# A RetNet layer and an RWKV channel mix on one core: the hand-written order of all instructions behind the first score products is replaced by another one

## The chip, the core and the metric

The kernel runs on one core of one Trainium2 chip. The metric is the device time of one execution in microseconds (us); a kernel is run several times and the median counts. Engines: PE is TensorE, DVE is VectorE, ACT is ScalarE, POOL is GpSimd, SP is SyncE.

## The reference

A decaying recurrent attention gives `x`, and a channel mix with a gate works on it. Batch 4, 8 heads, 768 tokens, head width 64, model width 512, inner width 1024.

```python
def _attn_ref(q, k, v):
    gamma = 1.0 - 2.0 ** (-5.0 - np.arange(H))
    for t in range(S):
        state = gamma * state + outer(k[:, :, t], v[:, :, t])   # per batch and head
        y[:, :, t] = 1/sqrt(D) * q[:, :, t] @ state

def _moe_ref(x, mu_k, mu_r, w_k, w_v, w_r):
    x_prev = x shifted by one token, zeros first
    xk = mu_k * x + (1.0 - mu_k) * x_prev
    xr = mu_r * x + (1.0 - mu_r) * x_prev
    k = np.maximum(xk @ w_k, 0.0)
    v = k * k @ w_v
    r = 1.0 / (1.0 + np.exp(-(xr @ w_r)))
    return r * v
```

## The kernel before

The 4 x 768 tokens are cut into 12 blocks of 256 tokens, three to a batch (blocks 0 to 2 are batch 0, and so on). A block goes through two parts. In the first the recurrence is done in chunks: q and k are turned, scores are made within a chunk and masked, and a state is summed and handed to the next block of the same batch. The second part mixes each token with the one before it, multiplies by `w_k`, takes relu and square, multiplies by `w_v`, and gates the result with a sigmoid of the product with `w_r`. Blocks 3 and 4, 6 and 7, 9 and 10 go through the mix and the product with `w_k` as pairs (`GROUPS`), so their product is 512 tokens wide and one word K stands for both.

There is no loop over blocks and no scheduler. The text `ORDER` lists some 620 words, each of which issues one step; the program walks it from left to right (the last loop of the kernel) under a manual schedule. Each engine and each DMA queue executes its own steps strictly in the order of the text, and waits, in the order of its queue, for what the step at its head depends on: its inputs, and that the buffer or PSUM bank it writes has been read by its last user. So the relative place of two words on one engine decides which of them can hold up the other. A word is `code.arguments`, then `~v`, `~a`, `~p` or `~s` for an engine (DVE, ACT, POOL, SP), then `@` and the PSUM banks. The codes that matter here, with the line of the step in the profile:

- `lq lk lv` (lines 265, 270): load q, k, v of a block; on POOL's queue except two on SP. Q and K have rings of four buffers, so `lv.10` needs `vs.6` to be done. `wk wr wv`: the weights, in parts.
- `tq tk` (L388): DMA transposes of q and k on SP's queue, for blocks 8 to 11. Blocks 0 to 7 use PE: `Tq Tk` (L343, 348, 354), copied out of PSUM by `Eq Ek` on ACT (L276).
- `vs` (L291, DVE): v scaled. `S` (L412, 425, 433, PE): scores. `M` (L457, DVE): mask. `C` (L469, 487, PE): products of k and v for the state. `U` (L522, DVE): the state's running sum. `G` (L527 ACT, L531 DVE): its decay.
- `I`, `Y`, `J` (L544, 574, 590, 601, PE): what the carried state and the masked scores give to the output. `sy` (L276, ACT): a small read of the output's bank.
- `D` (L633, 640, DVE): the attention's result leaves PSUM. `dx` (L655, DVE): difference to the token before. `X.n.0.j` and `X.n.1.j` (L681, DVE): the mix for `w_k` and for the gate, one quarter of the width each.
- `K` (L695 pairs, L705 single, PE): product with `w_k`. `Qa` (L727, ACT): relu. `Qb` (L741, L745, ACT): square. `R` (L754, PE): product with `w_r`. `s` (L760, ACT): sigmoid. `V` (L766; `Vc` L784 at the very end, PE): product with `w_v`, in two halves. `O` (L772; `Oc` L791, DVE): the result. `st` (L779; `sc` L799, on SP's queue, the last on ACT's): the store, from a ring of four buffers.
- `z` (L840, 847, PE): products of zeros, into a bank whose content is not used, placed where PE would have nothing to do. The argument counts quarter passes.

Of the kernel before, what the change touches and what calls it, by code (L numbers as in the profile page):

```python
# [50 lines left out]
Qb.2.1~a X.2.1.3 U.4.2 V.1.0.0@3 M.4 V.0.0.1 U.4.3 dx.3~v Tq.7@67 I.4@45 V.0.1.1 lq.11~p sy.4~a  # L51
O.0.0 Y.4 st.0.0 O.0.1 V.1.0.1 D.4~v lk.6~p st.0.1 R.2.0@2 O.1.0 V.1.1.1 s.2.0 lk.7~p dx.4~v
Eq.7~a V.2.0.0@1 O.1.1 Tk.5@23 Tq.5@67 lv.6~p X.3.0.0 Tq.6@45 R.2.1@0 X.3.0.3 Eq.6~a X.3.0.2
V.2.0.1 Ek.5~a lv.7~p X.3.0.1 V.2.1.0@4 G.4~a vs.5~v V.2.1.1 Eq.5~a X.3.1.3 K.3.7@5 lq.10~p s.2.1
# [14 lines left out]
K.6.0@5 Qa.6.5~a D.8~v Qb.6.1~a R.6.0@7 Qb.6.7~a dx.8~v R.7.1@4 K.6.3@2 O.5.0 s.7.1 Qa.6.0~a  # L69
X.8.0.3 R.6.1@3 X.8.0.0 Qb.6.0~a X.8.0.2 R.7.0@6 Qa.6.3~a X.8.0.1 U.9.0~a K.8.2@2 s.6.1 U.9.1  # L70
X.8.1.1 Qb.6.3~a K.8.3@3 U.9.2 Qa.8.2~a X.8.1.0 Qb.6.5~a K.8.1@5 vs.11~v s.7.0 V.6.1.0@2 s.6.0
U.9.3 Qa.8.1~a G.9~v C.10@01 X.8.1.3 Qa.8.3~a I.9@67 S.9@45 U.10.0~v V.6.1.1 Qb.8.3~a M.9 K.8.0@3
O.6.1 V.6.0.0@4 U.10.1 Qa.8.0~a st.6.1 U.10.2 st.5.0 Qb.8.2~a S.10@23 tq.11~s U.10.3 Y.9 Qb.8.0~a
M.10 I.10@01 Qb.8.1~a V.7.0.0@5 sy.10~a st.5.1 D.9~v V.6.0.1 tk.11~s V.8.1.0@2 X.8.1.2 dx.9~v Y.10
C.11@67 V.8.1.1 D.10~v V.8.0.0@3 dx.10~v V.8.0.1 V.7.0.1 X.9.0.2 R.8.1@0 X.9.0.3 X.9.0.1 V.7.1.0@1
s.8.1 X.9.0.0 V.7.1.1 O.8.1 K.9.7@0 O.6.0 st.8.1 G.10~v K.9.0@2 O.7.1 U.11.0~v K.9.5@4 Qa.9.0~a
O.7.0 K.9.2@1 X.9.1.2 Qb.9.0~a st.7.0 st.6.0 Qa.9.7~a X.9.1.1 K.9.1@5 U.11.1 X.9.1.0 K.9.6@0
Qa.9.1~a X.9.1.3 Qb.9.7~a R.8.0@2 Qa.9.6~a K.9.3@5 s.8.0 Qb.9.1~a R.10.0@0 O.8.0 Qa.9.2~a U.11.2
# [861 lines left out]
```

## Time and profile before

| | |
|---|---|
| median of 3 runs | 154.9 us (153.5, 154.9, 155.57) |
| the profiled execution | 153.46 us, of which its span 151.7 us |
| mean granted TensorE clock | 0.993 |
| PE busy | 142.4 us, 94% of the span |
| DVE busy | 126.7 us, 84% |
| ACT busy | 90.5 us, 60% |
| POOL busy | 61.2 us, 40% |
| DMA | 24.39 MB, mean 161 GB/s |

The span runs from the first to the last instruction of the program that the profiler recorded. Busy shares of PE count a matmul until its modelled end, so a busy PE is not PE at its peak. In rows of groups the columns are the line, the engine, the operation, out<-in, the shape and the count, then the busy time and the mean duration of one in ns, then the engine's idle time before them and who ended it. A row of the timeline has its start and its length in us, and in brackets the idle time before it and its releaser; several instructions of a kind are merged, with their count behind the x. "issue" as a releaser is time in which the engine waited for nothing that the profile shows. A row of stages has the stretch, its length, then busy time and number of instructions of each engine, the granted clock, the DMA share and the traffic. A row of the chain has start, length and what ran.

### The profile page before, as it was taken

To read this page: it belongs to the slowest core of one execution; us is meant where nothing else is said; L and a number is where in the kernel's file an instruction comes from. 1 tells how busy PE (TensorE), PEld (TensorE's weight loads), DVE (VectorE), ACT (ScalarE), POOL (GpSimd) and SP (SyncE) were. 2 spreads that over 40 slices of the span, in tenths; PEclk is the share of its full clock that TensorE was granted. 3 is DMA by queue.
4 is the path that set the end of the run, shared out by engine and by line. 5 is a ranking of instruction groups with operands and counts; after the bars stand their busy time and mean duration, and the time that the engine had idled before them with its cause. 6 is when DMAs were issued, how large, how long until landed. Compare 5 with 4: busy or idle time off the path is not lost.

```text
span 151.7 us, 5268 instructions
## 1 busy us (share of the span) xinstructions
PE 142.4 (94%) x2285; PEld 81.1 (53%) x2285; DVE 126.7 (84%) x208; ACT 90.5 (60%) x176; POOL 61.2 (40%) x76
## 2 busy tenths in 40 slices
...
GB/s 142 249 239 192 181 240 235 163 195 211 197 191 193 178 170 249 249 257 216 160 189 222 236 107 267 167 6 4 117 179 58 69 138 138 6 0 0 114 167 138
DMA packets 57599, 24.39 MB, mean 161 GB/s; under 512 B 49128, under 2 KB 53096, under 8 KB 57576
## 3 DMA queue, kind: packets, MB, share of 16 engines
...
q8 instruction: 18, 0.29, 0.8%
q10 hardware_dynamic: 432, 0.32, 0.7%
...
## 4 chain that ended last, share of the span: by engine, by line
PE 63%; DMA 15%; DVE 12%; issue 4%; POOL 3%; ACT 0%; DVEq 0%; POOLq 0%
PE ps L766 23%; PE ps L695 11%; PE ps L754 10%; DMA v<-in_v_dram 10%; PE ps L705 9%; DMA wk<-in_moe_w_k_dram 5%; DVE dx L655 2%; DVE xk L681 2%; PE ps L544 2%; PE ps L469 2%; DVE a L457 2%; PE ps L574 2%; PE ps L343 1%; PE ps L412 1%; DVE xr L681 1%
## 5 line engine op out<-in xcount | busy, mean ns | idle before, releaser
L766 PE MATMUL ps<-wv,k2s 128*128 128x512 f16 x184 | 43.0, 379 | 0.0
L727 ACT ACTIVATE kr<-ps 128x512 f32<-128x512 f32 x48 | 28.1, 596 | 22.8 <-PE ps L695 12.9
L766 PEld LDWEIGHTS <-k2s 128*128 128x128 f16 x184 | 17.4, 98 | 19.5 <-issue 0.2
L754 PE MATMUL ps<-wr,xr 128*128 128x512 f16 x96 | 23.4, 379 | 0.0
L705 PE MATMUL ps<-xk,wk 128*128 128x256 f16 x192 | 22.8, 273 | 0.4 <-DVE xk L681 0.4
L695 PE MATMUL ps<-xk,wk 128*128 128x512 f16 x96 | 22.7, 380 | 0.0
L457 DVE TENSOR_TENSOR a<-ps,c_sb 128x1024 f16<-128x1024 f32 (+1 forms) x18 | 19.5, 1099 | 3.7 <-PE ps L412 3.6
L760 ACT ACTIVATE rs<-ps 128x512 f32<-128x512 f32 x24 | 13.8, 608 | 13.9 <-PE ps L754 13.6
L772 DVE SCALAR_TENSOR_TENSOR os<-ps,rs 128x512 f32<-128x512 f32 x23 | 15.4, 685 | 6.7 <-DMA out_dram<-os 4.7
L705 PEld LDWEIGHTS <-wk 128*128 128x128 f16 x192 | 18.4, 98 | 4.1 <-DVE xk L681 0.5
L270 POOL DMA_DIRECT2D v<-in_v_dram x20 | 17.9, 919 | 6.0 <-DVE vs L291 4.6
L681 DVE SCALAR_TENSOR_TENSOR xr<-dx,mu,xT 128x256 f16<-128x256 f32 (+1 forms) x36 | 19.6, 566 | 0.1
L681 DVE SCALAR_TENSOR_TENSOR xk<-dx,mu,xT 128x256 f16<-128x256 f32 (+1 forms) x36 | 18.6, 567 | 0.1
L270 POOL DMA_DIRECT2D k<-in_k_dram x20 | 17.8, 917 | 1.4 <-DMA v<-in_v_dram 0.9
L291 DVE TENSOR_TENSOR vs<-v,csm_sb 128x1024 f16<-128x1024 f32 x12 | 14.6, 1217 | 3.2 <-DMA v<-in_v_dram 3.2
L741 ACT ACTIVATE k2s<-kr 128x512 f16<-128x512 f32 x24 | 14.8, 632 | 0.2
L655 DVE TENSOR_TENSOR dx<-xT 128x1024 f32<-128x1024 f32 x12 | 14.6, 1220 | 0.1
L695 PEld LDWEIGHTS <-wk 128*128 128x128 f16 x96 | 9.0, 98 | 10.3
L754 PEld LDWEIGHTS <-xr 128*128 128x128 f16 x96 | 9.0, 98 | 9.9
L745 ACT ACTIVATE k2s<-kr 128x512 f16<-128x512 f32 x24 | 14.1, 630 | 0.2
L633 DVE TENSOR_TENSOR xT<-ps,gy_sb 128x512 f32<-128x512 f32 x16 | 11.0, 689 | 2.3 <-PE ps L544 1.2
L270 POOL DMA_DIRECT2D q<-in_q_dram x10 | 9.0, 921 | 7.1 <-PE ps L343 6.8
...
## 6 DMA issues: line engine op xcount, KB each, us to landing
out_dram<-os SPq DMA_DIRECT2D x23, 256.0 KB, 4.0
v<-in_v_dram POOLq DMA_DIRECT2D x20, 256.0 KB, 6.6
k<-in_k_dram POOLq DMA_DIRECT2D x21, 128.0 KB, 6.9
q<-in_q_dram POOLq DMA_DIRECT2D x6, 256.0 KB, 8.7
q<-in_q_dram POOLq DMA_DIRECT2D x11, 128.0 KB, 6.6
v<-in_v_dram POOLq DMA_DIRECT2D x2, 512.0 KB, 6.9
wv<-in_moe_w_v_dram POOLq DMA_DIRECT2D x2, 512.0 KB, 9.2
wk<-in_moe_w_k_dram POOLq DMA_DIRECT2D x2, 256.0 KB, 8.8
```

Source lines behind the costliest of these rows:

```text
L270: e.dma_start(out=to[:, i, hs], in_=src[:, i])
L291: e.tensor_tensor(out=VS(n), in0=V32(n).rearrange("p (h i d) -> p i h d", i=2, h=H), in1=gks[:, int(half(n) or wide(n)), :, :, None].to_br ...
L457: nc.vector.tensor_tensor(out=dst, in0=dst if n in SPLITM else src, in1=mask[:, None, None, :].to_broadcast(list(dst.shape)), op=ALU.mult,)
L655: e.tensor_tensor(out=DX(k)[:, :, m * TM + t0 : m * TM + t1], in0=x[:, :, c + t0 : c + t1], in1=x[:, :, c - 1 + t0 : c - 1 + t1], op=ALU.s ...
L681: nc.vector.scalar_tensor_tensor(out=XM[w](k)[:, j, t0:t1], in0=DX(k)[:, j, t0:t1], scalar=mu[:, w * NCO + j : w * NCO + j + 1], in1=x[:, ...
L695: nc.tensor.matmul(banks("K", n, g), lhsT=wk16[:, co, g * P : g * P + P], rhs=XM[0](k)[:, co, :], start=(co == 0), stop=(co == NCO - 1),)
L705: nc.tensor.matmul(pz[:, i, :], lhsT=wk16[:, co, fo * P : fo * P + P], rhs=XM[0](k)[:, co, m * TM + t0 : m * TM + t1], start=(i == 0 and c ...
L727: nc.scalar.activation(out=kr, in_=banks("K", n, g, *u), func=AF.Relu)
L741: nc.scalar.activation(out=k2s[:, n % 3 : n % 3 + 2, g, :], in_=kr, func=AF.Square,)
L754: nc.tensor.matmul(banks("R", n, tb), lhsT=XM[1](k)[:, co, t : t + P], rhs=wr16[:, co, :], start=(co == 0), stop=(co == NCO - 1),)
L766: nc.tensor.matmul(banks("V", n, tb), lhsT=K2(n)[:, fo, tb * P : tb * P + P], rhs=wv16[:, fo, :], start=(fo == 0), stop=(fo == NFO - 1),)
L772: nc.vector.scalar_tensor_tensor(out=OS(2 * n + tb), in0=banks("V", n, tb), scalar=1.0 / (KSC * KSC), in1=RS(2 * n + tb), op0=ALU.mult, op ...
```

## The change

All words from the second line of the first score products on stand in another order, and many have other PSUM banks. The operations are the same ones with the same operands, and the loads are kept: each engine has the same work, with these exceptions. The zero products in the changed part have the counts 2, 2, 8 and 1 in place of 4, 3 and 5, and two more of the small reads `sy` are made on ACT (blocks 7 and 11). POOL's queue has its loads in the same sequence up to block 6; behind `lv.7` it goes on with `lq.8` and `lk.8` ahead of `lv.10`. SP's queue has `tk.9 tk.8 tq.8 tq.9` where it had `tq.8 tk.8 tq.10`, and its stores in another order. The diff, cut to the front, the two stretches around blocks 5 to 8, and the end:

```diff
@@ -35,54 +35,54 @@
 lq.0.0.2~s lk.0.0.2~s lv.0~p mu~s lk.0.2.4~p gy.0~v lq.0.2.4~p lv.1~p cq.0.0.2~a lk.1~p z.8@7
 Tq.0.0.2@0 ck.0.0.2~a lq.1~p Eq.0.0.2~a lq.2~p z.3@7 Tk.0.0.2@1 Ek.0.0.2~a wk.1~p gy.1~a z.3@7
 S.0.0.0.2@01 S.0.1.0.2@23 vs.0~v Tk.0.2.4@4 M.0.0.0.2 Ek.0.2.4~a z.1@7 Tq.0.2.4@5 lk.2~p C.0@67
-M.0.1.0.2 Eq.0.2.4~a U.0.0~v z.1@4 S.0.1.2.4@45 I.0@23 U.0.1 S.0.0.2.4@01 M.0.1.2.4 G.0~a
-M.0.0.2.4 vs.1~v wk.0~p z.4@6 Y.0 mt@0 Tk.1@1 D.0~v me C.1@45 Ek.1~a Tq.1@0 U.1.0~v dx.0~v Eq.1~a
-U.1.1 z.3@7 I.1@01 S.1.1@23 X.0.0.3 Tq.2@4 M.1.1 S.1.0@67 lv.2~p Eq.2~a M.1.0 wr~p X.0.0.0 z.5@5
-Y.1 X.0.0.1 X.0.0.2 Tk.2@6 D.1~v K.0.3@7 Ek.2~a X.0.1.2 lv.3~p Qa.0.3~a S.2.0@01 dx.1~v S.2.1@45
-G.1~a K.0.2@7 X.0.1.0 Qb.0.3~a K.0.0@6 X.1.0.2 Qa.0.2~a X.1.0.0 lq.3~p X.1.0.1 K.0.1@2 Qa.0.0~a
-X.0.1.3 X.1.0.3 Qb.0.2~a X.0.1.1 K.1.1@3 M.2.1 lk.3~p K.1.2@6 Qa.1.1~a vs.2~v K.1.3@7 Qb.1.1~a
-lk.4~p Qa.1.2~a X.1.1.0 K.1.0@3 Qa.1.3~a X.1.1.3 M.2.0 C.2@7 Qa.1.0~a lq.4~p R.0.1@6 Qb.1.2~a
-U.2.0~v Qb.0.0~a X.1.1.1 I.2@01 Y.2 vs.3~v sy.2~a Qb.1.0~a lv.4~p J.2 Tq.3@7 Qa.0.1~a D.2~v
-R.0.0@3 s.0.1 Eq.3~a wv.0~p X.1.1.2 C.3@45 Tk.3@6 dx.2~v U.3.0~a R.1.1@7 Qb.1.3~a lq.7~p Ek.3~a
-U.3.1 R.1.0@2 wv.1~p X.2.0.2 X.2.0.3 s.1.1 lk.5~p S.3.0@45 X.2.0.1 s.0.0 S.3.1@01 X.2.0.0 Tq.4@67
-s.1.0 X.2.1.2 K.2.0@3 Eq.4~a M.3.1 lq.5~p K.2.1@2 Qa.2.0~a vs.4~v Qb.0.1~a K.2.2@0 Qa.2.1~a lv.5~p
-G.3~a Tk.4@67 M.3.0 I.3@23 K.2.3@1 sy.3~a Ek.4~a X.2.1.1 Y.3 Qa.2.2~a C.4@67 J.3 S.4@45 Qa.2.3~a
-U.4.0~v V.1.1.0@0 D.3~v Qb.2.2~a Qb.2.0~a V.0.0.0@1 lq.6~p X.2.1.0 Qb.2.3~a U.4.1 V.0.1.0@2
...
-O.2.0 K.3.6@6 O.2.1 Qa.3.7~a X.3.1.2 C.5@01 st.2.1 Qa.3.6~a S.5@45 st.1.1 U.5.0~v Tk.6@23 st.1.0
-X.3.1.0 K.3.2@6 Ek.6~a X.3.1.1 K.3.0@7 Qb.3.7~a U.5.1 vs.6~v K.3.3@2 Qa.3.0~a Qb.3.6~a R.4.0@3
-U.5.2 lv.10~p Qa.3.3~a M.5 K.3.5@7 s.4.0 Qa.3.2~a vs.7~v I.5@23 S.6@45 lv.8~p sy.5~a C.6@01 Y.5
-M.6 U.6.0~a Qb.3.2~a K.3.4@6 Qb.3.0~a lv.9~p D.5~v R.4.1@4 Qa.3.4~a Qb.3.3~a K.3.1@5 U.6.1
...
-st.2.0 I.7@67 G.7~v S.7@01 st.3.0 R.5.1@5 tq.8~s M.7 V.5.1.0@2 s.5.1 dx.6~v tk.8~s Y.7 C.8@01
-D.7~v R.5.0@5 tq.10~s V.4.0.0@3 dx.7~v V.5.0.0@6 U.8.0~v V.4.1.1 X.6.0.0 V.5.1.1 U.8.1 X.6.0.3
-V.4.0.1 X.6.0.1 V.5.0.1 X.6.0.2 O.4.0 K.6.4@7 O.4.1 K.6.2@3 X.6.1.0 Qa.6.4~a st.4.1 tq.9~s U.8.2
-K.6.7@4 Qa.6.2~a O.5.1 Qb.6.4~a K.6.6@7 X.6.1.3 Qa.6.7~a tk.9~s X.6.1.1 I.8@23 S.8@01 Qa.6.6~a
-X.6.1.2 K.6.1@4 Qb.6.6~a tk.10~s M.8 K.6.5@7 Qa.6.1~a s.5.0 vs.10~v Y.8 st.4.0 Qb.6.2~a C.9@01
...
-V.9.0.1 O.10.1 O.10.0 K.11.0@4 X.11.1.3 K.11.1@2 X.11.1.0 Qa.11.0~a O.9.0 K.11.3@0 X.11.1.2
-Qa.11.1~a X.11.1.1 V.9.1.1 Qa.11.3~a Qb.11.1~a K.11.2@2 O.9.1 Qb.11.0~a R.11.0@0 Qb.11.3~a st.9.1
-st.9.0 Qa.11.2~a R.11.1@3 st.10.1 s.11.0 st.10.0 Qb.11.2~a V.11.0.0@2 s.11.1 V.11.0.1 Vc.11.1.0@3
-O.11.0 Vc.11.1.1@0 st.11.0 Oc.11.1.0 sc.11.1.0~s Oc.11.1.1 sc.11.1.1~a
+M.0.1.0.2 Eq.0.2.4~a U.0.0~v z.1@4 S.0.0.2.4@45 I.0@23 U.0.1 S.0.1.2.4@01 M.0.0.2.4 mt@6 me G.0~a
+M.0.1.2.4 z.2@4 Tk.1@4 vs.1~v wk.0~p Y.0 Ek.1~a Tq.1@5 D.0~v C.1@01 Eq.1~a U.1.0~v dx.0~v z.2@7
+I.1@45 S.1.1@23 S.1.0@67 U.1.1 M.1.1 G.1~a lv.2~p M.1.0 X.0.0.1 z.8@0 Y.1 wr~p X.0.0.3 X.0.0.0
+Tq.2@6 X.0.0.2 Tk.2@7 Eq.2~a D.1~v K.0.2@2 Ek.2~a lv.3~p X.0.1.2 K.0.3@6 dx.1~v Qa.0.2~a S.2.1@45
+S.2.0@01 Qb.0.2~a X.0.1.3 K.0.1@7 X.1.0.0 X.1.1.3 lq.3~p K.0.0@2 X.1.0.3 Qa.0.1~a X.1.0.1 Qa.0.3~a
+X.1.0.2 X.1.1.1 Qb.0.1~a z.1@3 K.1.2@3 X.1.1.0 lk.3~p Qa.0.0~a vs.2~v K.1.0@6 Qa.1.2~a Qb.0.3~a
+K.1.1@7 M.2.0 lk.4~p Qb.1.2~a C.2@3 Qb.0.0~a X.0.1.0 K.1.3@2 Qa.1.0~a X.1.1.2 X.0.1.1 lq.4~p
+R.1.1@6 U.2.0~v Qa.1.3~a M.2.1 Qa.1.1~a I.2@23 sy.2~a Qb.1.0~a Tq.3@7 lv.4~p vs.3~v Y.2 Eq.3~a J.2
+R.0.1@4 D.2~v wv.0~p s.1.1 Tk.3@5 Qb.1.1~a C.3@67 dx.2~v lq.7~p R.0.0@2 U.3.0~a Ek.3~a wv.1~p
+U.3.1 R.1.0@3 X.2.0.1 lk.5~p s.0.0 X.2.0.2 S.3.1@67 s.0.1 X.2.0.3 Tq.4@01 X.2.0.0 s.1.0 Tk.4@45
+X.2.1.3 Qb.1.3~a K.2.0@2 lq.5~p X.2.1.2 Eq.4~a M.3.1 K.2.1@3 Qa.2.0~a vs.4~v S.3.0@01 lv.5~p
+Qa.2.1~a K.2.3@2 Ek.4~a M.3.0 K.2.2@3 G.3~a X.2.1.1 C.4@45 S.4@01 Qa.2.3~a U.4.0~v I.3@67 Y.3
+sy.3~a Qa.2.2~a M.4 V.0.1.0@2 Qb.2.3~a Qb.2.1~a lq.6~p U.4.1 V.0.0.0@3 U.4.2 U.4.3 J.3 X.2.1.0
+I.4@01 V.1.1.0@4 sy.4~a D.3~v Y.4 dx.3~v Tq.7@67 V.0.1.1 Eq.7~a lq.11~p D.4~v V.1.1.1 Qb.2.2~a
...
+V.2.0.0@2 lv.7~p G.4~a X.3.0.2 V.2.0.1 X.3.1.3 Eq.6~a K.3.1@3 vs.5~v lq.8~p s.2.1 K.3.6@6 Qa.3.1~a
+O.1.0 C.5@01 X.3.1.1 st.1.0 Tk.6@45 lk.8~p st.0.1 K.3.4@3 U.5.0~v Ek.6~a X.3.1.2 K.3.3@7 U.5.1
+Qa.3.4~a O.2.0 R.3.0@4 Qa.3.3~a U.5.2 vs.6~v Qa.3.6~a S.5@01 Tk.7@23 s.3.0 I.5@67 Qb.3.3~a M.5
+K.3.5@5 sy.5~a lv.10~p Ek.7~a R.3.1@4 Qb.3.4~a vs.7~v C.6@23 lq.10~p s.3.1 Y.5 S.6@01 Qa.3.5~a
+D.5~v R.4.0@4 Qb.3.6~a lv.8~p Qb.3.1~a K.3.0@5 s.4.0 dx.5~v K.3.7@6 Qa.3.0~a Qb.3.5~a V.2.1.0@7
...
+V.3.1.1 U.7.0~v lk.10~p O.3.0 K.5.0@4 U.7.1 st.3.0 O.3.1 st.2.0 V.4.1.0@7 st.2.1 Qa.5.0~a U.7.2
+lk.11~p st.3.1 U.7.3 tk.9~s I.6@45 I.7@01 vs.8~v sy.6~a R.5.1@6 sy.7~a G.7~v Y.6 tk.8~s Y.7 D.6~v
+V.4.0.0@2 tq.8~s K.5.3@3 D.7~v V.4.1.1 Qa.5.3~a tq.9~s dx.6~v Qb.5.1~a R.5.0@4 s.5.1 R.4.1@3
+Qb.5.0~a dx.7~v Qb.5.3~a V.4.0.1 s.5.0 vs.10~v s.4.1 V.5.1.0@6 X.6.0.2 C.8@45 V.5.1.1 X.6.0.1
...
+Qb.9.5~a K.11.0@2 s.9.1 K.11.2@7 s.9.0 V.10.1.0@4 V.10.0.1 R.11.1@6 K.11.1@1 K.11.3@0 Qa.11.1~a
+V.9.0.1 Qa.11.3~a Qa.11.0~a V.10.1.1 O.9.0 Qa.11.2~a V.9.1.0@2 O.10.0 Qb.11.1~a st.9.0 Qb.11.2~a
+V.9.1.1 Qb.11.3~a Qb.11.0~a R.11.0@5 O.9.1 V.11.0.0@7 O.10.1 st.9.1 s.11.0 st.10.0 s.11.1 V.11.0.1
+st.10.1 Vc.11.1.0@6 O.11.0 Vc.11.1.1@5 st.11.0 Oc.11.1.0 sc.11.1.0~s Oc.11.1.1 sc.11.1.1~a
 """
```

More of the change, by code (lines that the diff above doesn't have):

```diff
@@ L49 @@
-G.3~a Tk.4@67 M.3.0 I.3@23 K.2.3@1 sy.3~a Ek.4~a X.2.1.1 Y.3 Qa.2.2~a C.4@67 J.3 S.4@45 Qa.2.3~a
-U.4.0~v V.1.1.0@0 D.3~v Qb.2.2~a Qb.2.0~a V.0.0.0@1 lq.6~p X.2.1.0 Qb.2.3~a U.4.1 V.0.1.0@2
[L51 to L54, printed above, removed]
@@ L67 @@
-K.6.7@4 Qa.6.2~a O.5.1 Qb.6.4~a K.6.6@7 X.6.1.3 Qa.6.7~a tk.9~s X.6.1.1 I.8@23 S.8@01 Qa.6.6~a
-X.6.1.2 K.6.1@4 Qb.6.6~a tk.10~s M.8 K.6.5@7 Qa.6.1~a s.5.0 vs.10~v Y.8 st.4.0 Qb.6.2~a C.9@01
[L69 to L78, printed above, removed]
```

29 lines of the change are left out of this document (21 added, 8 removed).

## The prediction

> **What bounds the kernel now.** I read the page first, then the busy time by stage, then TensorE's groups from the first product with `wv` to the last matmul, then the timeline around single words of the order.
>
> ```profile
> span 151.7 us, 5268 instructions
> PE 142.4 (94%) x2285; PEld 81.1 (53%) x2285; DVE 126.7 (84%) x208; ACT 90.5 (60%) x176; POOL 61.2 (40%) x76
> ...
> q8 instruction: 18, 0.29, 0.8%
> ```
>
> ```profile
> core 0: us, PE busy (x) PEld busy (x) DVE busy (x) ACT busy (x) POOL busy (x), PEclk, DMA share, GB/s
> 20.00:42.90 22.90, 21.49 (x385) 15.86 (x379) 21.03 (x33) 19.71 (x41) 18.01 (x21) 1.00 1.55 205
> 42.90:64.90 22.00, 22.00 (x417) 10.99 (x416) 21.64 (x33) 13.66 (x26) 12.05 (x14) 1.00 1.56 207
> 64.90:66.30 1.40, 0.70 (x83) 0.59 (x72) 1.40 (x2) 0.05 (x1) 1.40 (x3) 1.00 0.90 245
> 66.30:97.00 30.70, 30.64 (x544) 16.95 (x534) 29.62 (x48) 19.73 (x39) 14.70 (x17) 1.00 1.57 205
> 97.00:125.00 28.00, 27.98 (x374) 14.98 (x373) 26.92 (x45) 13.68 (x28) 0.00 (x0) 1.00 0.34 83
> 125.00:147.40 22.40, 22.36 (x218) 12.49 (x216) 11.23 (x20) 13.34 (x26) 0.00 (x0) 1.00 0.20 72
> ```
>
> From 42.9 us on PE is busy throughout at the full clock; the one stage with a hole is 64.9 to 66.3. DVE is nearly full until 125 and then has half its time free, so PE has a backlog at the end: any us that PE loses after 42.9 is a us on the span. But busy includes the pipeline's tail, so I sum what PE needs by start-to-start times from the chain:
>
> ```profile
> L766 PE MATMUL ps<-wv,k2s 128*128 128x512 f16 x184 | 43.0, 379 | 0.0
> L695 PE MATMUL ps<-xk,wk 128*128 128x512 f16 x96 | 22.7, 380 | 0.0
> L754 PE MATMUL ps<-wr,xr 128*128 128x512 f16 x80 | 19.4, 379 | 0.0
> L705 PE MATMUL ps<-xk,wk 128*128 128x256 f16 x96 | 11.5, 273 | 0.0
> ```
>
> ```profile
> 101.61 2.62 PE ps L705 x24
> ...
> 112.18 0.38 PE ps L574 x32
> ...
> 113.13 3.56 PE ps L766 x16
> ...
> 119.28 5.18 PE ps L695 x24
> ```
>
> The groups give the counts in that stretch (xcount), the chain's rows the time of so many in a row. A 512-wide product takes 5.18/24 = 0.216 us, a 256-wide one 2.62/24 = 0.109, a 64-wide one 0.38/32 = 0.012 or a little less. So 360 x 0.216 = 77.8, 112 (the 96 and the last 16) x 0.109 = 12.2, and some 1,160 small ones (the stages' counts less the dense) x 0.011 = 12.8: 102.8 us in a stretch of 104.5. At most about 1.7 us is to be had behind 42.9; 0.70 of it is one wait, of which more below. Before 42.9 stands the front, and behind 147.4 a tail of 4.3. The order can thus gain little unless V, the product with `wv`, starts sooner.
>
> **The sum's base.** The profiled execution took 153.46 us, 1.76 beside its span. The median of the three runs is 154.9, so this execution is 1.4 below it. I add to 153.46.
>
> **The front (to the first V).** The loads keep their sequence on POOL up to block 6 and set fixed points:
>
> ```profile
> 22.91 1.79 POOL L270 DMA_DIRECT2D q<-in_q_dram  x2
> ...
> 31.90 0.78 POOL L879 DMA_DIRECT2D wv<-in_moe_w_v_dram  x1
> ...
> 32.54 1.23 DVE L640 TENSOR_TENSOR xT<-ps,gy_sb 128x1024 f32<-128x1024 f32 x1 [0.48 <-ACT k2s L745]
> ...
> 34.21 1.22 DVE L655 TENSOR_TENSOR dx<-xT 128x1024 f32<-128x1024 f32 x1
> ...
> 35.67 1.66 DVE L681 SCALAR_TENSOR_TENSOR xk<-dx,mu,xT 128x256 f16<-128x256 f32 x4
> ...
> 37.09 1.07 ACT L276 COPY qT<-ps 128x1024 f16<-128x1024 f16 x1
> ...
> 37.39 2.79 PE L705 MATMUL ps<-xk,wk 128*128 128x256 f16 x24 [0.37 <-DVE xk L681]
> ...
> 39.92 1.21 DVE L457 TENSOR_TENSOR a<-ps,c_sb 128x1024 f16<-128x1024 f32 x1
> ...
> 42.89 4.49 PE L766 MATMUL ps<-wv,k2s 128*128 128x512 f16 x20
> ```
>
> ```profile
> L522 DVE TENSOR_TENSOR tg<-ps,tg 128x256 f16<-128x256 f32 x24 | 10.1, 419 | 1.7 <-PE ps L544 1.2 <-ACT tg L527 0.2 <-ACT tg L276 0.2
> ```
>
> The page's last part, from issue to landing, of these two loads:
>
> ```profile
> q<-in_q_dram POOLq DMA_DIRECT2D x2, 128.0 KB, 7.4
> ...
> wv<-in_moe_w_v_dram POOLq DMA_DIRECT2D x1, 512.0 KB, 8.1
> ```
>
> The first half of `wv` lands at 31.9 + 8.1 = 40.0, so V could start 2.9 earlier; it does not, because DVE's queue holds block 2 back. Before: D.2 at 32.54, one gate mix X.1.1.2, dx.2, U.3.1, four X.2.0, and K.2 at 37.39. After, X.1.1.2 stands ahead of D.2 (one 0.40 more there, 1.66/4) and D.2 waits no more for the settling copy, which moves ahead of Y.2: D.2 at about 32.8, then 1.14 + 1.14 + 0.34 + 4 x 0.40 = 4.2 (D, dx and U from 1.23, 1.22 and 0.42, each less the 0.08 by which rows of a full queue overlap), the last X.2.0 at 37.1: K.2 starts 0.2 sooner. From there to V PE has four K.2 (each 8 x 0.109), C.4 and S.4 (each 32 small ones, 0.38 at most) and S.3.0, I.3 and Y.3 (28 wider ones, together about 0.9): 5.1. It loses 0.3 at K.2.3, since Eq.4 (1.07) now runs on ACT just before the Qa.2.0 that frees the bank, and 0.3 at S.4 for M.3.0's bank: V at 42.8 against 42.89. J.3 (0.15) is still to do. **Term: -0.1**, from -0.7 (neither wait arises) to +1.0 (both grow as the Eq copy slides).
>
> The zero products change from 12 to 13 quarter passes, all in this front; there PE waits for DVE, whose queue is full (21.03 of 22.9), so they cost nothing. Without that cover one pass is 0.2.
>
> **The middle.** The one visible wait:
>
> ```profile
> 64.64 0.45 PE L412 MATMUL ps<-qT,kT 64*64 64x64 f16 x32
> ...
> 64.89 0.22 PE L469 MATMUL ps<-vs,k 64*64 64x64 f16 x4
> ...
> 65.82 0.41 PE L469 MATMUL ps<-vs,k 64*64 64x64 f16 x28 [0.70 <-issue]
> ```
>
> No engine released it. The page lists 18 instruction transfers; 4,570 PE records over 18 are 254 each, so a fresh block begins about every 254. Counting matmuls with their loads along the order, blocks that begin at this C.6 also begin inside S.2.1, where the trace has another short issue wait; both times PE is racing through 64-wide products, here behind I.5 and S.6 (48 products, some 0.6 us). My reading is a late instruction block. In the new order the same count falls in C.6 again, but behind K.3.5 and R.3.1, 1.73 us of dense work; and in no other place does a boundary follow more than one small word. **Term: -0.7**, bounds -0.7 and +0.7 (it moves or doubles). The Trainium skill, "Runtime: NRT & Kernel Launch", section "Instruction fetch mechanics", says that crossing a 16 KiB block is mostly hidden. By that rule the 0.70 has another cause that the reorder need not remove, the term is 0 and the sum 153.3; the row with no releaser is nearer to my reading.
>
> Handoffs between DVE and PE: I summed each queue's work from the first V in both orders. Before, PE arrives ahead of DVE at S.6 (0.4), K.6.4 (0.65), Y.8 (0.9). After, it does so between blocks 3 and 5 (C.5, S.5, up to 0.3 once V starts at 42.8), and behind K.5 DVE is always ahead, by 0.4 to 5 us. Deficits do not add, since a PE wait moves all later ones. **Term: 0**, from -0.6 to +1.0. The changes from dense to small words grow from 15 to 17, at 0.1 each (the 3.56 of the row above, behind small ones, less 16 x 0.216): **+0.2**.
>
> **The tail.**
>
> ```profile
> 146.77 0.69 DVE L772 SCALAR_TENSOR_TENSOR os<-ps,rs 128x512 f32<-128x512 f32 x1 [4.69 <-DMA out_dram<-os]
> ...
> out_dram<-os SPq DMA_DIRECT2D x3, 256.0 KB, 4.0
> ```
>
> O.11.0 waits for the store of block 9 whose buffer it reuses, and pushes the two half results behind it by 0.3. After, that store leaves some 4 us sooner; the other store of block 9 (needed by the last half) leaves about 4 us before its use, just its own 4.0. **Term: -0.3**, bounds -0.3 and +0.3.
>
> **Sum:** 153.46 - 0.1 - 0.7 + 0 + 0.2 - 0.3 = 152.6, 1.5% below the median shown. A change of 2% (151.8 or 158.0) is about what a measurement of this kernel can tell from none.
>
> **Rivals.** *Faster (B):* the favourable ends together. V at 42.2 (-0.7), the 1.7 us of slack in the middle all gone, the tail -0.3, changes +0.2: 151.0. For it: later slacks of 0.4 to 5 us, and that the median carries 1.4 more than this profile. Against it: part of the 1.7 is the 0.1 a change, which stays.
>
> *Slower, by the load of q for block 3 (C):* on PE Tq.3 now stands ahead of Y.2; before it stood behind. It needs the second half of that load: the two issues span 22.91 to 24.70, so it lands at 23.8 + 7.4 = 31.2, and Y.2's mask is ready at about 31.65. If the load comes d us later, Y.2, J.2, D.2 and all of block 2 move by d - 0.4 with no work behind it in PE's queue that could go instead. Beyond d = 2.7 the time is over 154.9; at d = 4 it is 156.2. For it: the DMA is saturated there (share 1.55). Against it: the loads' sequence is kept.
>
> *Slower, by the transposes (D):*
>
> ```profile
> 63.41 3.54 POOL L270 DMA_DIRECT2D v<-in_v_dram  x4 [4.55 <-DVE vs L291]
> ...
> 84.33 3.07 SPq L388 DMA_TRANSPOSE kT<-k  x1
> ...
> 93.11 0.44 PE L412 MATMUL ps<-qT,kT 64*64 64x64 f16 x32
> ```
>
> ```profile
> qT<-q SPq DMA_TRANSPOSE x1, 9.0
> ...
> k<-in_k_dram POOLq DMA_DIRECT2D x2, 128.0 KB, 11.0
> ```
>
> Block 8's are now second and third on SP, behind tk.9 and the store of O.3.1 at about 76, while loads run to 77 (18 issues of 0.89, 3.54/4, from vs.6 at 61.3; four block-8 loads fill POOL's 4.55 hole ahead of it). The third leaves two issues of 3.07 later, near 82.3, and lands by 91.3 with 9.0; I.8 stands near 92.6, a slack of 1.3. The loads beside a transpose took 11.0 instead of about 7; if transposes stretch as much (9.0 to 14.1), I.8 waits 3.8: 156.4. It beats the gain from 2.3 us late on. The Trainium skill, "DMA: Bandwidth & Descriptors", section "Issuing engines are not separate DMA queues", says that all issuers share the same 16 engines and interleave, which speaks for D; the 11.0 agrees.
>
> *Nothing moves:* the stalls only change place and the time is 154; this lies inside my forecast's own spread.
>
> **Chances.** Forecast (151.8 to 155) 0.44, B 0.32, C 0.13, D 0.11. Faster by 2%: B and a little, 0.34. Slower by 2%: C or D with more delay than priced, or both, 0.16. Within: 0.50. The range goes from B's 151.0 less 0.4 to C and D with half a us more: 150.6 to 156.9. The forecast's own range is 151.8 to 155.
>
> **What would show it.** Right: V's first row near 42.8 and K.2 near 37.2; no issue wait of over 0.4 on PE behind it; O.11.0 released by PE; DVE's idle time between 66 and 125 grows while PE's stages stay full. Wrong: V later than 43.5 with Tq.3 or Y.2 waiting for q (C); PE or its loads waiting for qT or kT near 92 (D); a span below 150 with V near 42 (B).

## The result, and the profile after

| | before | after |
|---|---|---|
| median of 20 runs | 154.19 us (153.03 to 155.82) | 155.28 us (154.07 to 157.99) |
| ratio after/before | | 1.0074, 95% interval 1.0049 to 1.0100 |
| profiled execution | 153.46, span 151.7 | 154.50, span 152.7 |

The change makes the kernel 0.5 to 1.0% slower. The two profiled executions differ by 1.0 us; both lie below the medians. A ratio counts only the fast executions of a kernel (none in the slower state, none over 1.5% above its fastest), while a median counts all. The page of after:

```profile
span 152.7 us, 5280 instructions
PE 143.9 (94%) x2286; PEld 81.4 (53%) x2286; DVE 127.3 (83%) x208; ACT 90.4 (59%) x178; POOL 61.3 (40%) x76
...
q8 instruction: 18, 0.29, 0.8%
```

Its stages, cut at the first V, around C.6, and at the last matmul:

```profile
20.00:42.95 22.95, 22.43 (x415) 16.62 (x404) 22.48 (x37) 19.20 (x35) 18.31 (x22) 1.00 1.54 206
42.95:64.40 21.45, 21.19 (x423) 10.69 (x419) 20.94 (x30) 14.46 (x28) 13.84 (x16) 1.00 1.70 211
64.40:65.40 1.00, 0.15 (x19) 0.10 (x16) 0.44 (x1) 1.00 (x3) 1.00 (x2) 1.00 1.91 220
65.40:97.00 31.60, 31.55 (x499) 16.97 (x499) 29.25 (x47) 17.53 (x37) 13.38 (x16) 1.00 1.41 203
97.00:125.00 28.00, 28.00 (x481) 15.51 (x480) 27.03 (x44) 13.77 (x27) 0.00 (x0) 1.00 0.41 87
125.00:148.70 23.70, 23.64 (x193) 12.91 (x191) 13.28 (x25) 14.08 (x28) 0.00 (x0) 1.00 0.19 71
```

The hole in PE is still there, at 64.4 to 65.4 instead of 64.9 to 66.3, and the DMA share in the stage ahead of it is 1.70 instead of 1.56. PE's timeline of after, at K.2, the first V, J.3, Tq.5, C.6 (two rows) and I.8:

```profile
37.60 1.91 PE L705 MATMUL ps<-xk,wk 128*128 128x256 f16 x16
...
42.95 1.90 PE L766 MATMUL ps<-wv,k2s 128*128 128x512 f16 x8
44.78 0.42 PE L544 MATMUL ps<-qT,tg 64*64 64x128 f16 x20
...
52.69 0.45 PE L343 MATMUL ps<-c_sb,q 64*64 64x64 f16 x32 [0.17 <-ACT rs L760]
...
64.17 0.28 PE L469 MATMUL ps<-vs,k 64*64 64x64 f16 x11
65.30 0.37 PE L469 MATMUL ps<-vs,k 64*64 64x64 f16 x21 [0.85 <-issue]
...
96.22 0.33 PE L544 MATMUL ps<-qT,tg 64*64 64x64 f16 x16
```

DVE at O.0.0, D.5 and O.11.0:

```profile
51.26 0.69 DVE L772 SCALAR_TENSOR_TENSOR os<-ps,rs 128x512 f32<-128x512 f32 x1
...
66.23 0.69 DVE L633 TENSOR_TENSOR xT<-ps,gy_sb 128x512 f32<-128x512 f32 x1 [1.39 <-PE ps L544]
...
146.98 0.69 DVE L772 SCALAR_TENSOR_TENSOR os<-ps,rs 128x512 f32<-128x512 f32 x1 [1.36 <-ACT rs L760]
```

C.6 stops after 11 of its 32 products with no releaser, 0.85 long where before had 0.70. Numbered from 0 in order of time, the matmul that waits is **number 1117 in both orders**: after 4 products of C.6 in before, after 11 in after.

To see the rest I take PE's time from the start of the first V to the end of the last matmul: 104.47 us in before, 105.68 in after. 0.07 of the 1.21 between them is J.3, which after still has to do there. Then I add up how much longer each PE word takes, from its first product to that of the next word, than the lower quartile of its kind in the two kernels together. The two sums differ by 1.15, and 0.93 of that has arisen by 63 us, ahead of C.6. The largest parts in after are the wait at Tq.5 (0.33; none in before), Y.4 (0.28; 0.12 in before) and Tk.6 (0.25; 0.12 in before); the rest is spread over many small ones. C.6 itself differs by 0.15. Tq.5's bank is freed by s.2.0, which waits for a place in its ring of four until O.0.0 is done:

```profile
52.04 0.60 ACT L760 ACTIVATE rs<-ps 128x512 f32<-128x512 f32 x1 [3.18 <-DVE os L772]
```

### The profile page after: what moved, and what is told of

The parts are those of the page before. It is cut to its first block, busy times and chain, and to the rows that moved or that the text cites. A ratio compares the mean times of both kernels' runs of the same rounds, so it can differ in the third digit from the quotient of the medians.

```text
span 152.7 us, 5280 instructions
## 1 busy us (share of the span) xinstructions
PE 143.9 (94%) x2286; PEld 81.4 (53%) x2286; DVE 127.3 (83%) x208; ACT 90.4 (59%) x178; POOL 61.3 (40%) x76
## 4 chain that ended last, share of the span: by engine, by line
PE 64%; DVE 22%; issue 5%; DMA 4%; ACT 1%; DVEq 0%; ACTq 0%; POOLq 0%
PE ps L766 18%; PE ps L754 12%; PE ps L705 11%; PE ps L695 11%; DMA v<-in_v_dram 4%; DVE xk L681 4%; DVE a L457 4%; DVE dx L655 3%; DVE xT L633 3%; DVE xT L640 2%; DVE os L772 2%; PE ps L544 2%; PE ps L412 2%; PE ps L469 2%; PE ps L343 2%
## 5 line engine op out<-in xcount | busy, mean ns | idle before, releaser
L705 PE MATMUL ps<-xk,wk 128*128 128x256 f16 x192 | 23.6, 273 | 0.4 <-DVE xk L681 0.2
L695 PEld LDWEIGHTS <-wk 128*128 128x128 f16 x96 | 9.1, 98 | 10.8 <-issue 0.3
L741 ACT ACTIVATE k2s<-kr 128x512 f16<-128x512 f32 x24 | 14.3, 634 | 0.1
L745 ACT ACTIVATE k2s<-kr 128x512 f16<-128x512 f32 x24 | 14.1, 630 | 0.1
```

The source lines that it names most:

```text
L695: nc.tensor.matmul(banks("K", n, g), lhsT=wk16[:, co, g * P : g * P + P], rhs=XM[0](k)[:, co, :], start=(co == 0), stop=(co == NCO - 1),)
L705: nc.tensor.matmul(pz[:, i, :], lhsT=wk16[:, co, fo * P : fo * P + P], rhs=XM[0](k)[:, co, m * TM + t0 : m * TM + t1], start=(i == 0 and c ...
```

## The experiments

Ratios are to runs of before on the same chip. Lag is the time from matmul 989 (one block of 128 matmuls ahead of 1117) to the start of the next 16 KiB instruction transfer; the times of single transfers are from the trace's transfer records. The lags and waits are collected in a table at the end.

**Where in the order?** Three hybrids: one order up to a word, behind it the remaining words in the other's sequence.

```
h_front_after    words of after  ... V.0.1.0 | rest as before
h_front_before   words of before ... V.0.1.0 | rest as after,  I.4@01 -> I.4@34
h_mid_after      words of after  ... C.6     | rest as before, 7 banks renamed
h_mid_before     words of before ... C.6     | rest as after,  6 banks renamed
```

h_front_after: 

> After up to the word ahead of V.0.1.0, behind it the order of before, with no bank renamed. Theory A (after's loss lies behind the first V, in waits of TensorE for banks and for DVE at Y.4, Tq.5 and Tk.6, 0.8 in all): 0.1 to 0.4 over before, near 154.4. Rival C (the front's state is the cause): near 155.2.

h_front_before: 

> Before up to the word ahead of V.0.1.0, behind it the order of after (one pair of banks renamed). Theory A: after's front is worth only 0.2 of the 1.1 (V 0.06 later, J.3 still to do 0.15), so 0.8 to 1.0 over before, near 155.1. Rival C (the front is the cause, by the lag that it leaves on DVE): near before, 154.2.

h_mid_after: 

> The order of after up to the word ahead of C.6, then the words left over in the order of before (7 banks renamed). Theory A (the loss lies between the first V and C.6: PE lost 1.52 us over its nominal work by 63 in after against 0.68 in before): about 0.9 to 1.1 us over before, so near 155.2, as after. Rival B (the loss comes behind C.6, from the late transposes and the block-by-block V words): no more than 0.3 over before, near 154.3.

h_mid_before: 

> The mirror: before up to the word ahead of C.6, then the words left over in the order of after (6 banks renamed, Qb.3.3 a place earlier so that the KR ring holds). Theory A: within 0.3 of before, or below it by the shorter tail (0.27), so 153.8 to 154.4. Rival B: 0.9 to 1.1 over before, near 155.2.

Measured: h_front_after 1.0020 (0.9985 to 1.0055), h_front_before 1.0139 (1.0097 to 1.0181), h_mid_after 1.0436, h_mid_before 1.0469. After's front alone costs nothing that can be told; by its interval it is 0.55% at most, so the front does not carry the whole loss. The other three are poor tests, for the seam made waits of its own. PE's rows behind it in h_front_before, h_mid_after and h_mid_before:

```profile
46.50 0.65 PE L544 MATMUL ps<-qT,tg 64*64 64x64 f16 x16 [0.92 <-DVE a L457]
```

```profile
77.64 0.37 PE L544 MATMUL ps<-qT,tg 64*64 64x64 f16 x10 [2.02 <-DVE t L522]
```

```profile
74.76 0.40 PE L705 MATMUL ps<-xk,wk 128*128 128x256 f16 x1 [4.23 <-DVE xk L681]
```

In the first the renamed bank makes I.4 wait for a mask; in the others PE has no dense word left to cover DVE's sums and mixes. From the C.6 hybrids nothing follows on the loss.

**A place in the stream, or the word's own data?**

```
-X.0.0.1 z.8@0 Y.1
+X.0.0.1 z.4@0 n.33@0 Y.1        n: products of 64x64 by 64 zeros
```

> After with 33 products of 64x64 by 64 zeros in the front in place of one of the two 128x512 zero products ahead of Y.1, where PE idles: 32 matmuls more in PE's instruction stream and nothing else. Theory F (the 0.85 us wait at C.6 is a late block of instructions: in both traces it stands at matmul 1117 of the stream): the wait moves to the same number in the stream, so out of C.6 to a place 32 matmuls earlier in the order, near 62 us, and grows, since the block ahead of it is then used up in 4.0 us rather than 5.6: to about 2.5 us, perhaps with a second wait one block on; 2 to 3.5 us slower than after. Rival G (the wait is C.6's own, for its data): still 0.85 at C.6, the time that of after.

Measured: 1.0449 (1.0394 to 1.0504). PE's rows at Tk.2 and I.5:

```profile
22.35 0.82 PE L354 MATMUL ps<-c_sb,k 128*64 128x128 f16 x14 [2.17 <-issue]
```

```profile
64.73 0.25 PE L544 MATMUL ps<-qT,tg 64*64 64x64 f16 x4
66.83 0.39 PE L544 MATMUL ps<-qT,tg 64*64 64x64 f16 x12 [1.85 <-issue]
```

The wait left C.6 for I.5, the place that is now number 1117, and grew to 1.85: it belongs to the stream of instructions, and rival G falls. It was smaller than the 2.5 expected. The time (161.2) was larger, for two reasons. The 33 small products also made such a wait in the front, 2.17 at number 350, where I had expected none; V began at 45.8. And right behind each of the two waits the granted clock was 0.5 for 3.4 us (from 22.5 and from 66.9 us).

**More work in the block ahead.**

```
after_r40    -R.3.1@4 ... C.6@23 ... S.6@01 Qa.3.5~a D.5~v R.4.0@4
             +R.3.1@4 ... R.4.0@0 C.6@23 ... S.6@14 Qa.3.5~a D.5~v
before_r41   -S.6@45 ... C.6@01 Y.5 ... K.3.4@6 ... R.4.1@4
             +S.6@45 ... R.4.1@6 C.6@01 Y.5 ... K.3.4@4
after_again  after, unchanged
```

after_r40: 

> After with one dense word, R.4.0, moved from behind S.6 to ahead of C.6 (R.4.0 into bank 0, S.6 into banks 1 and 4, K.3.2 into bank 0). Theory F (the block of instructions that begins at matmul 1117 comes some 6.5 us after the crossing into the block ahead of it, and the 128 matmuls of that one are used up in 5.6): with 0.87 us more work in them the wait at 1117 falls from 0.85 to under 0.2, and the time by 0.5 to 0.9, to near 154.5. Rival H (the wait follows the order: C.6 must wait for what it needs): the wait stays at 0.8 or grows, the time that of after or more.

before_r41: 

> Before with one dense word, R.4.1, moved from behind K.3.4 to ahead of C.6 (R.4.1 into bank 6, K.3.4 into bank 4). Theory F: the wait of 0.70 at matmul 1117 falls to under 0.2, and the time by 0.3 to 0.7, to 153.3 to 153.8, unless the next block, used up 0.87 sooner, comes late in its turn. Rival H: no gain.

after_again: 

> After, unchanged, a second look. Theory F: the wait at matmul 1117 is there again, 0.5 to 1.2 us, since the order makes it and not chance; the time 1.004 to 1.010 of before. Rival I (the wait differs from run to run with the load on the DMA engines): it is gone or over 1.5 us, and the time moves with it.

Measured: after_r40 1.0036 (0.9997 to 1.0075), before_r41 1.0033 (0.9998 to 1.0067), after_again 1.0108 (1.0056 to 1.0161). C.6 in after_again:

```profile
64.20 0.28 PE L469 MATMUL ps<-vs,k 64*64 64x64 f16 x11
66.70 0.37 PE L469 MATMUL ps<-vs,k 64*64 64x64 f16 x21 [2.22 <-issue]
```

This execution was the slowest of its six, 157.59 us where their median is 155.80. Its stage behind the wait shows why:

```profile
67.80:71.20 3.40, 3.40 (x9) 1.22 (x10) 3.23 (x5) 0.60 (x1) 3.40 (x5) 0.50 1.54 221
```

The granted clock was 0.5 for these 3.4 us. R.4.0 and K.3.0, which run there, took 0.8 longer each than elsewhere. So the long wait is 1.4 of the 3.1 us by which it lies above the profiled execution of after, and the low clock 1.6.

In before_r41, at S.6 and C.6:

```profile
66.43 0.45 PE L412 MATMUL ps<-qT,kT 64*64 64x64 f16 x32 [0.47 <-DVE a L457]
...
67.77 0.45 PE L469 MATMUL ps<-vs,k 64*64 64x64 f16 x32
```

In before_r41 C.6 runs through, as expected, but S.6 now waits 0.47 for a mask and nothing is gained. In after_r40 the wait stayed, 0.84, with another of 0.78 at number 989: the transfer began 5.2 us after the crossing, where I had reckoned with a fixed time. And the same kernel had 0.85 in one profile and 2.22 in the next, with lags of 4.32 and 5.75. So theory F holds for the place and fails for the size: rival I is right that the size varies. That also fits after's wider spread (154.07 to 157.99, before 153.03 to 155.82). What makes the transfer late?

**The loads in flight.** POOL's timeline of after, ahead of the transfer (62.87 to 63.84):

```profile
56.15 1.84 POOL L270 DMA_DIRECT2D q<-in_q_dram  x2
57.89 0.97 POOL L270 DMA_DIRECT2D k<-in_k_dram  x1
59.47 0.88 POOL L270 DMA_DIRECT2D k<-in_k_dram  x1 [0.61 <-DMA k<-in_k_dram]
62.88 1.78 POOL L270 DMA_DIRECT2D v<-in_v_dram  x2 [2.53 <-DVE vs L291]
```

In before POOL issued two such loads there, lq.10, and then stood idle from 58.9 to 63.41. After puts lq.8 and lk.8 there, four.

```
after_swap    -lv.7 ... lq.8 ... lk.8 ... lv.10 ... lq.10 ... lv.8
              +lv.7 ... lq.10 ... lv.10 ... lq.8 lk.8 ... lv.8
before_swap   -lv.7 ... lq.10 ... lv.10 lv.8 lv.9 lk.9 lk.8 lq.8
              +lv.7 ... lk.8 lq.8 ... lv.10 lv.8 lv.9 lk.9 lq.10
before_lq10   -lv.7 ... lq.10 ... lv.10 lv.8 lv.9 lk.9
              +lv.7 ... lv.10 lv.8 lv.9 lq.10 lk.9
after_late    -lv.7 ... lq.8 ... lk.8 ... lv.10 ... lq.10 ... lv.8
              +lv.7 ... lv.10 ... lv.8 lq.8 lk.8 lq.10
```

after_swap: 

> After with one thing of POOL's queue put back: lq.10 in the place of lq.8 and lk.8, and these two behind lv.10, so that nothing is issued between 59 and 62.9 us, as in before. Theory L (the block of instructions from matmul 1117 on comes late because its DMA stands behind the loads in flight: it began 4.3, 5.8 and 5.2 us after the crossing at 989 in three looks at after's order, and 4.0, 3.8 and 4.2 in three at before's): its start comes near 4.0 after the crossing, the wait at 1117 falls to 0.3 to 0.8, and the time to 1.003 to 1.006 of before. Rival J (the wait comes from the order of the words on TensorE alone): unchanged, 1.007 to 1.011, wait 0.85 to 2.2.

before_swap: 

> Before with the same thing of after alone: lk.8 and lq.8 in the place of lq.10, and lq.10 where they stood. Theory L: the block's DMA begins some 5 us after the crossing at 989 instead of 4.0, the wait at 1117 grows from 0.70 to 1.3 to 2.0, and the time by 0.5 to 1.2, to 1.003 to 1.008. Rival J: the time of before.

before_lq10: 

> Before with lq.10 moved behind lv.9 on POOL's queue: nothing is issued from 56.7 to 63.4 us. Theory L: the block's DMA begins 3 us or less after the crossing, the wait of 0.70 at 1117 is gone, and the time falls by 0.4 to 0.8, to 0.995 to 0.998. Rival J: the time of before, the wait as it was.

after_late: 

> After with lq.8, lk.8 and lq.10 all behind lv.8: nothing issued from 56.2 to 62.9 us. Theory L: the wait at 1117 gone (under 0.2), the time 0.8 to 1.5 below that of after, to 0.998 to 1.003 of before; what is left over before is the 0.5 of waits for banks at Y.4, Tq.5 and Tk.6. Rival J: unchanged from after.

Measured: after_late **0.9999** (0.9969 to 1.0029), before_swap **1.0070** (1.0034 to 1.0107), before_lq10 1.0003 (0.9972 to 1.0033), after_swap 0.9995 (0.9948 to 1.0042). POOL in after_late:

```profile
52.74 3.58 POOL L270 DMA_DIRECT2D v<-in_v_dram  x4
62.95 3.51 POOL L270 DMA_DIRECT2D v<-in_v_dram  x4 [6.63 <-DVE vs L291]
```

and PE there, at Tk.6 (number 989) and C.6 (number 1117):

```profile
58.99 0.34 PE L343 MATMUL ps<-c_sb,k 64*64 64x64 f16 x17 [0.27 <-issue]
...
65.18 0.37 PE L469 MATMUL ps<-vs,k 64*64 64x64 f16 x21 [0.30 <-issue]
```

Three words later on POOL's queue alone take after back to the time of before, and one swap on the same queue makes before as slow as after. So the place of these loads decides about the loss. The wait at 1117 fell from 0.85 and 2.22 to 0.30. That the loads act by way of this wait is less well shown. The profiled execution of after_late took 154.82 us, no less than after's 154.50: its wait at 1117 is 0.55 shorter, but it has 0.27 at number 989, 0.36 at S.11, and V 0.12 later, so the gain stands in the times. The profiled execution of before_swap was the shortest of its runs (154.0 where their median is 155.41) and shows 0.47 at 1117, no more than before. From the first V to the last matmul PE takes 105.25 us there, 0.8 more than in before; that lies in an issue wait at number 1373, the first of a later block, in one for DVE's sum at I.7, and in an issue wait at number 2012. after_swap is undecided: its ratio is 0.9995, but the median of its twelve runs is 155.44 where before's is 154.60. The profiled one, of 157.0, has a lag of 4.98, where theory L expected about 4.0, and a wait of 1.40; 1.5 us of its time lies ahead of the first V, where the granted clock was 0.5 from 10.8 to 17.6 us.

before_lq10 lost its wait at 1117 as expected (lag 2.19; C.6's 32 products in one row), but paid elsewhere:

```profile
65.18 0.47 PE L469 MATMUL ps<-vs,k 64*64 64x64 f16 x32
```

```profile
94.52 0.45 PE L412 MATMUL ps<-qT,kT 64*64 64x64 f16 x32 [1.79 <-DMA kT<-k]
```

S.8, right behind I.8, waits for the transposed k of block 8, which in before's order comes out of SP's queue with little to spare. Two variants to have the one without the other:

```
before_lq10b  lq.10 behind lq.8 (not behind lv.9)
before_tq8    and lk.9 behind lq.8;  -st.3.1 st.2.0 st.3.0 tq.8 tk.8
                                     +tq.8 tk.8 st.3.1 st.2.0 st.3.0
```

before_lq10b: 

> Before with lq.10 moved behind lq.8 on POOL's queue, so that the loads of block 8 keep their times (with lq.10 behind lv.9 the block's DMA began 2.2 us after the crossing at 989 and the wait at 1117 was gone, but tq.8 and tk.8 came 2 us later and I.8 waited 1.8). Theory L: no wait at 1117 and less than 1.8 at I.8: 0.3 to 0.9 under before, 0.994 to 0.998. Rival K (the loads end as late in all, and the transposes wait for the last of them, not for their own): I.8 waits 1.5 to 1.8 again, the time that of before.

before_tq8: 

> The same, with lk.9 behind lq.8 too, and tq.8 and tk.8 ahead of st.3.1 on SP's queue, so that they go out when lq.8 has landed, near 76, before the last loads. Theories L and K alike: no wait at 1117 and none at I.8, 0.6 to 1.1 under before, 0.993 to 0.996.

Measured: before_lq10b 1.0054 (1.0018 to 1.0090), before_tq8 1.0161 (1.0079 to 1.0242). S.8 in the first, K.6.2 in the second:

```profile
94.20 0.45 PE L412 MATMUL ps<-qT,kT 64*64 64x64 f16 x32 [1.11 <-DMA kT<-k]
```

```profile
92.40 0.81 PE L695 MATMUL ps<-xk,wk 128*128 128x512 f16 x3 [2.65 <-DVE os L772]
```

Both expectations failed. In the first the transposes are late all the same (1.11, under rival K's 1.5 to 1.8), and the wait at 1117 was back (0.54, lag 3.70) though the same loads were in flight as in before_lq10 with 2.19; that difference stays open. In the second the block's wait is gone and the transposes come in time, but O.4.0 waits for st.2.0, now behind them on SP, and K.6.2 for O.4.0's bank.

**Is the wait at Tq.5 lost, or only moved?**

```
-O.0.1 V.1.0.0@5 dx.4~v R.2.0@2 lk.7~p O.0.0 V.1.0.1
+O.0.1 V.1.0.0@5 O.0.0 dx.4~v R.2.0@2 lk.7~p V.1.0.1
after_late_o, after_late_o2: on top of after_late;  after_o00: on after
after_tk6: after_late_o and Tk.6@45 -> @47, K.3.3@7 -> @5
```

after_late_o: 

> After with its three loads late, as in the run before, and O.0.0 ahead of dx.4 on VectorE, so that s.2.0 finds its place in the ring 1.2 us sooner. Theory A (the 0.33 that Tq.5 waits for the bank of R.2.0 is lost for good): 0.2 to 0.4 under the kernel with the late loads alone. Theory F: the wait at Tq.5 goes, but TensorE then waits as much longer for vs.5 and O.1.0 at C.5 and Tk.6 or for the block at matmul 989: within 0.15 of it.

after_late_o2: 

> The kernel with the late loads and O.0.0 ahead of dx.4 once more. If its 0.9935 is the order's and not chance: 0.990 to 0.997 of before again, and no wait of over 0.3 at matmul 1117. If the wait there comes back with chance as it does in after (0.85 and 2.22 in two looks): over 0.997, and the wait is seen.

after_o00: 

> After with O.0.0 ahead of dx.4 alone, its loads where after has them. With the late loads this step was worth some 0.6% (0.9935 against 0.9999 of before). If the two steps add (theory A): 0.6 to 1.0 us under after, 1.001 to 1.005 of before. If TensorE, 0.33 sooner at the crossing of 989, only waits as much longer for the block at 1117 behind the same loads (theory L): the time of after, 1.006 to 1.011, and a wait of over 1 us at 1117.

after_tk6: 

> The kernel with the late loads and O.0.0 ahead of dx.4, and Tk.6 in banks 4 and 7 (K.3.3 in 5), so that it needn't wait 0.44 for O.1.0. Theory A: 0.2 to 0.4 under that kernel, 0.990 to 0.992 of before. Theory F: the block at 1117 had 0.22 us to spare in that kernel, so the gain is 0.1 to 0.25 and the rest comes back there as a wait.

Measured: after_late_o **0.9935** (0.9900 to 0.9971), median 153.41; after_late_o2 **0.9959** (0.9927 to 0.9991), median 153.36; after_o00 0.9986 (0.9946 to 1.0026), median 155.02; after_tk6 0.9964 (0.9932 to 0.9996). PE in after_late_o, at Tq.5 and C.6:

```profile
51.75 0.45 PE L343 MATMUL ps<-c_sb,q 64*64 64x64 f16 x32
...
63.45 0.45 PE L469 MATMUL ps<-vs,k 64*64 64x64 f16 x32
```

The kernel is faster than before in two separate measurements. The wait at Tq.5 counts, and the step brought more than its 0.33. In the profiles st.0.0 leaves at 50.14 instead of 52.09, the transfer ahead of number 989 began 2.2 and 3.2 us after its crossing instead of 3.7, and the waits at 989 and 1117 are gone as well (0.27 and 0.30 before the step). Part of that is chance: V starts at 42.26 and 42.38 instead of 43.07, though the order up to there is the same. On after with its early loads (after_o00) Tq.5's wait is gone too, and C.6 is held 1.12, as theory L said. But the interval lies wholly under the 1.006 to 1.011 that theory L gave for the time, and holds part of theory A's range, so the step brings time there as well. Tk.6's other bank gained nothing: K.3.4 behind it then waits for Ek.6:

```profile
59.53 1.02 PE L695 MATMUL ps<-xk,wk 128*128 128x512 f16 x4 [0.17 <-ACT kT L276]
```

**The block that begins at matmul 1117 in the profiles** (us; the transfer is the one between the two crossings):

| kernel | 989 at | transfer | lag | 1117 at | wait | 1117 less transfer's end |
|---|---|---|---|---|---|---|
| before | 59.38 | 63.40-64.34 | 4.01 | 65.82 | 0.70 | 1.48 |
| before_swap | 59.30 | 63.22-64.18 | 3.93 | 65.44 | 0.47 | 1.26 |
| before_lq10b | 59.43 | 63.13-64.22 | 3.70 | 65.62 | 0.54 | 1.40 |
| h_front_after | 60.58 | 64.41-65.37 | 3.83 | 66.78 | 0.39 | 1.41 |
| before_r41 | 60.61 | 64.83-65.79 | 4.22 | 67.77 | none | |
| before_lq10 | 59.74 | 61.93-63.02 | 2.19 | 65.23 | none | |
| before_tq8 | 59.60 | 61.64-62.72 | 2.03 | 65.09 | none | |
| after | 58.55 | 62.87-63.84 | 4.32 | 65.30 | 0.85 | 1.46 |
| after_again | 58.59 | 64.33-65.30 | 5.75 | 66.70 | 2.22 | 1.40 |
| after_r40 | 59.01 | 64.22-65.18 | 5.21 | 66.58 | 0.84 | 1.40 |
| after_o00 | 58.70 | 63.40-64.36 | 4.70 | 65.72 | 1.12 | 1.36 |
| h_front_before | 59.21 | 63.65-64.62 | 4.44 | 66.05 | 0.96 | 1.43 |
| shift32 | 60.95 | 64.19-65.40 | 3.24 | 66.83 | 1.85 | 1.43 |
| after_swap | 60.51 | 65.49-66.45 | 4.98 | 67.81 | 1.40 | 1.36 |
| after_late | 58.99 | 62.79-63.85 | 3.80 | 65.18 | 0.30 | 1.33 |
| after_late_o | 57.85 | 60.80-61.87 | 2.95 | 63.54 | none | |
| after_late_o2 | 57.97 | 60.57-61.66 | 2.60 | 63.66 | none | |
| after_tk6 | 58.04 | 60.51-61.69 | 2.46 | 64.08 | none | |

The two hybrids at C.6 are left out: with lags of 5.50 and 3.66, and 7.9 and 6.4 us between the crossings, neither has a wait at 1117. Where PE waits it goes on 1.3 to 1.5 us after the transfer's end, in every row; the transfer takes about 1. So the block is there about lag + 2.4 after the crossing, and PE waits for what it needs less than that for 128 matmuls.

## Why the prediction was wrong

152.6 was forecast, 0.9 below the profiled execution of before; after's took 154.50, 1.0 above it, and the medians moved by 1.1 in the same direction. Two terms of the sum failed, by about the same amount: the wait at C.6 (forecast -0.7, measured +0.15) and the handoffs (forecast 0, measured some +0.9).

- **The bound** held in this: what PE loses behind the first V reaches the end (V 0.06 later, J.3's 0.07 still to do, 1.15 more over the usual time of the words; the last matmul ends 1.28 later, at 148.64 instead of 147.36). What the stretch could give was read too low. The 0.38 for 32 small products includes the 0.1 for the change from a dense word; elsewhere in before 32 take 0.28 (Y.4 from 48.80 to 49.08, Tk.5 from 52.88 to 53.16). With 0.009 for each, PE needs some 4 us less than the stretch, not 1.7; the changes are part of these 4.
- **The front** (-0.1): K.2 at 37.60 instead of 37.2, V at 42.95 instead of 42.8. J.3 came as foretold, but the term leaves it out. With it the front is +0.13. After's front alone (h_front_after) does not carry the loss.
- **The wait at C.6** (-0.7) is the first step that failed. The cause was named rightly, a late block. The step from there, that 1.73 us of dense work in front would hide it, was wrong: the boundary moved only by 7 products within C.6, and what counts is the work in the whole block of 128 matmuls against lag + 2.4. Without the wait that work took 5.7 us in before (59.38 to 65.82 less 0.70) and 5.9 in after (58.55 to 65.30 less 0.85). And the lag was longer, 4.32 instead of 4.01, with four early loads ahead of the transfer instead of two, which I had priced only against the transposes. Measured: +0.15 in one profile and +1.5 in the other, the second outside my bounds; it also lost 1.6 by the low clock behind the wait. After_late holds the loads back and returns 0.75% of the time; what sets the lag in a single execution stays open (after_swap, before_lq10b).
- **The handoffs** (0) are the second: some 0.9 was lost between V and C.6, near the upper bound of +1.0 (S.5 at 61.5). I had looked for PE ahead of DVE at C.5 and S.5 (0.3); what came were waits at Y.4 and for banks at Tq.5 and Tk.6. At Tq.5 DVE and ACT only stand in between (O.0.0, s.2.0). A sum per queue does not see rings of four. O.0.0 ahead of dx.4 removes the wait at Tq.5 and takes 0.4 to 0.6% off the time with the late loads.
- **Small words** (+0.2): not separable in these runs.
- **The tail** (-0.3) was right: O.11.0 is released by ACT's last sigmoid and no more by a store, and the time from the last matmul's end to the span's end is 4.10 instead of 4.33 (-0.23). Only its releaser I had named wrongly, as PE.
- **The rivals.** C did not come: Tq.3 starts at 31.47, as the load lands at 31.44, and Y.2 at 32.0, near the end of its mask (32.1). D did not come: I.8 at 96.22 waits for nothing. B's gain did not come either. Of the slower side I had the right resource, loads that delay another transfer, but had looked only at block 8's transposes and not at PE's own instructions.
- **The Trainium skill.** "Runtime: NRT & Kernel Launch", section "Instruction fetch mechanics", has the crossing of a 16 KiB block mostly hidden; 12 of the 18 profiles above have a wait at this one crossing, 0.30 to 2.22 us. "DMA: Bandwidth & Descriptors", section "Issuing engines are not separate DMA queues", has the transfers that ScalarE, SyncE and GpSimd start interleave on the same 16 engines; the section does not speak of instruction transfers. That these lag by up to 5.75 us while loads run fits a shared resource, but no run here shows which engines they use.

With the loads held back and O.0.0 moved, after_late_o and after_late_o2 take 0.9935 and 0.9959 of before. That this lies beside the forecast's ratio, 152.6/153.46 = 0.9944, is in part luck. In the profile of after_late_o PE takes 104.79 us from the first V to the last matmul, no less than before's 104.47: the wait at C.6 is gone, but those at Y.4 and Tk.6 (0.28 and 0.45) are not. It ends sooner because V starts at 42.26 and the tail is 0.23 shorter, and V's start lies between 42.26 and 43.07 in the profiles that have after's front at the full clock.
